# Stacked float32r products for a rank 32 term, with a tile of parts for each pair of heads

## The chip, the cores and the metric

One Trainium2 chip, one of its cores. The metric is the device time of one execution of the program in microseconds (us), the median over runs.

## The reference

Three layers follow one another; B = 4 sequences of S = 576 tokens, 512 features (8 heads of 64). The change touches the second line of the second layer.

```python
# 1: attention with a window of 128, ALiBi bias, per head
scores = where(mask, q @ k.T / 8 + bias, -1e9)
x = softmax(scores) @ v                       # [4, 576, 512]
# 2: low rank mix over the tokens, then a channel MLP
xt = x.transpose(0, 2, 1)
u = x + (xt @ U @ V).transpose(0, 2, 1)       # U [576, 32], V [32, 576]
x = u + maximum(u @ w_ch1, 0) @ w_ch2         # 512 -> 2048 -> 512
# 3: gated MLP
h = maximum(x @ w_in, 0); a, g = split(h)
out = (a * (w_spatial @ layernorm(g) + b_spatial)) @ w_out
```

## The kernel before, in words

Everything is written as tasks of a planner (`Plan`, L147): a task names its engine or a choice of engines, a cost, a priority and what it reads and writes. `run` (L216) lays the tasks out on TensorE (PE), VectorE (DVE), ScalarE (ACT), GpSimd (POOL) and the DMA queue of SP eight times, with priorities taken from the layout before, and emits the order that its own costs call the shortest. So a task that is added anywhere in the attention part can move the tasks around it on every engine, and a task with a choice (L599 `minus`, L413 `copy`, the normalisation at L1079) can change its engine. Within an engine the emitted order is the order of execution. Tiles live in rings of buffers (L109); a new tile of a ring waits for all users of the buffer's last tile.

The attention part goes through the sequences b = 0 to 3 and through four pairs of heads in each. `heads` (L996) loads q and k, computes scores (L1044), maximum and exponentials (L1055 on DVE, L1060 on ACT), normalises (L1080 on POOL or L1082 on DVE), transposes (L1090) and multiplies with v (L1128). `turned` (L1143) transposes the result once more (L1155). `low_rank` (L1162) then adds the low rank term to the sequence's tiles `u[b][pair]`, which hold features in the partitions and tokens in the columns:

- the mix (L1171) computes U^T x: 20 float32 products per sequence, whose results stand in one PSUM tile `t`, 32 rows for each pair;
- one copy (L1176, carried out at L416) brings `t` into the SBUF tile `th`;
- `up` (L1181) multiplies with V. `v32` holds V in each of the four groups of 32 rows, so that the products of all four pairs run at the same time in four groups of rows of the array (mode "quarter rows"). V's 576 columns are done in two halves of 288; the four products of one half are one task, here called a block. Each product is float32, which the trace shows as two instructions;
- VectorE adds each result to `u[b][pair]` (L1189).

In sequence 0 this is done for pairs 0 and 1 first, and later for pairs 2 and 3 (four half blocks, of two products each); in sequences 1 to 3 for all four pairs at once (two blocks each). The results lie in the PSUM rings `sc` and `at`, three buffers each (one more each in sequence 0); `t` is a buffer of `at` too.

`low_rank_weights` (L974) loads U and V as 64 bit words, turns them into float32 with five operations (L452 to L465) and spreads V over the rows with four DMAs (L983).

While attention is still going on, TensorE is filled with the first quarter of the channel MLP for the first 1536 tokens (`early_group`, L555): L545 to L547 for the first weight matrix, L584 to L586 for the second. These are float32r: each operand is split into a high and a low part that float32r holds exactly, and three products (high x high, low x high, high x low) stand for one. The three lines are called a triple. When attention is done its pool of SBUF is given back, and the casts (L529, ACT) and subtractions (L532, POOL) for the other tokens of that quarter may write there; their first product is L545 with 384 columns.

Of the kernel before, what the change touches and what calls it, by code (L numbers as in the profile page):

```python
# [338 lines left out]
def tile_kernel(ctx, tc, qT, kT, v, U, V, w1, w2, w_in, wspT, bsp, w_out, bias, out):  # L339
    nc = tc.nc  # L340
# [82 lines left out]
    def engines(kind, usual):  # L423
        return BOTH if kind in K["flex"] else (usual,)
# [512 lines left out]
    def constant(name, shape, dtype):  # L937
        return Ring(in_att, name, 1).new(shape, dtype)
# [25 lines left out]
    for p in ps:  # L964
        for t in (0, 8):
            P.add("POOL", 0.1, lambda p=p, t=t: nc.gpsimd.memset(p[:, REST[t] * 128 + 64 : REST[t] * 128 + 128], 0.0),
                  w=[p.part("zero")], prio=-1)
    r_xt, r_th = Ring(in_att, "xt", 2), Ring(in_att, "th", 2)


    u32 = constant("u32", [128, 5, RANK], F32)
    v32 = constant("v32", [128, S], F32)

    def low_rank_weights(prio, early, prio_v, early_v):  # L974
        single(u32, [(0, block(U, 0, 128, 0, RANK)), (1, block(U, 64, S, 0, RANK, 4))], 5, RANK, prio, None, early)
        P.add("DVE", 0.1, lambda: nc.vector.memset(u32[64:, 0], 0.0), w=[u32], prio=prio)
        n = S // 2
        v4 = constant("v4", [128, 1, n], F32)
        single(v4, [(0, block(V, 0, RANK, i // 2 * n, i // 2 * n + n), slice(RANK * i, RANK * i + RANK)) for i in range(4)],
               1, n, prio_v, None, early_v)  # L980
        for q in range(2):
            for d in range(2):
                P.dma(64, n, lambda q=q, d=d: nc.sync.dma_start(  # L983
                    out=v32[64 * d : 64 * d + 64, q * n : q * n + n], in_=v4[64 * q : 64 * q + 64, 0]),
                    r=[v4], w=[v32.part((q, d))], prio=K["vc"])

    vl = {}
    spare = r_f1.new([128, 128], F32)
# [173 lines left out]
    def low_rank(b, xts, pairs, p0):  # L1162

        sc, tp = (r_sc0, r_at0) if b == 0 else (r_sc, r_at)
        rows = slice(pairs[0] * 32, pairs[-1] * 32 + 32)
        t, th = tp.new([128, 128], F32), r_th.new([128, 128], F32)

        def mix():
            for c in range(5):
                for pair in pairs:  # L1170
                    nc.tensor.matmul(t[pair * 32 : pair * 32 + 32], u32[:, c], xts[pair // 2][:, c, pair % 2],  # L1171
                                     start=c == 0, stop=c == 4, skip_group_check=True)

        P.add("PE", 5 * 4 * 128 / 2400 + 0.1, mix, r=[u32] + [xts[h].part(c) for h in {p // 2 for p in pairs} for c in (0, 2, 4)],
              w=[t], prio=p0, mode="quarters")
        copy(engines("t", "ACT"), 128, lambda: th[rows], lambda: t[rows], PSUM, r=[t], w=[th], prio=p0 + 0.05)  # L1176
        for s0 in (0, 288):
            sl = slice(s0, s0 + 288)
            outs = [(sc, tp)[pair % 2].new([128, 288], F32) for pair in pairs]

            def up(sl=sl, outs=outs):  # L1181
                for pair, o in zip(pairs, outs):
                    d = slice(pair * 32, pair * 32 + 32)
                    nc.tensor.matmul(o.ap(), th[d], v32[d, sl], start=True, stop=True)

            P.add("PE", 4 * 288 / 2400 + 0.1, up, r=[th] + list(v32.parts.values()), w=outs, prio=p0 + 0.1, mode="quarter rows")
            for pair, o in zip(pairs, outs):
                ub = u[b][pair]
                P.add("DVE", dve(288), lambda o=o, ub=ub, sl=sl: nc.vector.tensor_tensor(  # L1189
                    out=ub[:, sl], in0=o.ap(), in1=ub[:, sl], op=ALU.add),  # L1190
                    r=[o], w=[ub.part(0), ub.part(1), ub], prio=p0 + 0.2)
# [544 lines left out]
```

## Time and profile before

| | us |
|---|---|
| median of 3 runs | 714.22 (714.04 to 715.3) |
| the profiled execution, its own time | 713.79 |
| its span, first to last instruction | 712.0 |
| TensorE busy | 701.7 (99%) |
| VectorE busy | 576.0 (81%) |
| ScalarE busy | 394.0 (55%) |
| GpSimd busy | 75.0 (11%) |

The granted TensorE clock is 1.00 over the span. PE is the matmul side of TensorE, PEld its weight loads; matmuls are pipelined and their recorded ends overlap the next one's start, so a product's price is read from start to start. VectorE's rows overlap in the same manner by a little.

### The profile page before, as it was taken

What the parts mean: (1) busy time and instruction counts of PE and PEld (TensorE: products, weight loads), DVE (VectorE), ACT (ScalarE), POOL (GpSimd) and SP (SyncE); (2) the same over time, 40 slices, a digit from 0 to 9 for tenths busy, and PEclk for the clock granted to TensorE, in tenths of its full rate; (3) what the DMA queues carried; (4) which work ended last, traced back from release to release, by engine and by line L of the source; (5) the groups of instructions that cost most, each with busy time, mean ns of one, the idle gap of its engine ahead of it and who ended that gap; (6) DMA issues with size and microseconds to landing.
All of it is one profiled execution on the core that took longest, in us unless ns stands there. A gap on an engine that the chain in (4) does not pass through costs nothing.

```text
span 712.0 us, 14829 instructions
## 1 busy us (share of the span) xinstructions
PE 701.7 (99%) x5434; PEld 637.8 (90%) x5434; DVE 576.0 (81%) x1637; ACT 394.0 (55%) x1082; POOL 75.0 (11%) x114
## 2 busy tenths in 40 slices
PE   8989999999999999999999999999999999999998
PEld 6767778778799999999999999999998898898896
DVE  6999996775597999999695998696589989859561
ACT  7878666564353655547253562544267566566352
POOL 2243330310400000000000000040010100100000
DMA  8865212210074166628475555447694202100102
GB/s 233 280 221 161 66 52 82 72 53 2 1 225 157 42 228 220 223 106 267 149 225 175 168 195 185 144 148 264 239 386 174 80 30 68 54 22 0 60 1 75
DMA packets 58799, 98.48 MB, mean 138 GB/s; under 512 B 8357, under 2 KB 38309, under 8 KB 58726
## 3 DMA queue, kind: packets, MB, share of 16 engines
q1 hardware_dynamic: 58437, 97.23, 41.2%
q8 instruction: 43, 0.70, 0.4%
q14 instruction: 31, 0.25, 0.1%
q10 hardware_dynamic: 288, 0.30, 0.1%
HBM read 67.67 MB, written 29.54 MB: 137 GB/s over the span
## 4 chain that ended last, share of the span: by engine, by line
PE 88%; DVE 7%; ACT 2%; DMA 1%; issue 1%; POOL 0%; SPq 0%; POOLq 0%; ACTq 0%
PE sc L586 8%; PE sc L584 8%; PE sc L585 8%; PE at L885 6%; PE at L886 6%; PE at L887 6%; PE at L1128 3%; PE sc L1044 2%; PE sc L1423 2%; PE sc L1421 2%; PE sc L1422 2%; PE at L1090 2%; PE at L1423 2%; PE at L1421 2%; PE at L1422 2%; PE acc L584 2%
## 5 line engine op out<-in xcount | busy, mean ns | idle before, releaser
L584 PE MATMUL sc<-h,wa 128*128 128x384 f32 (+1 forms) x328 | 110.6, 337 | 0.0
L585 PE MATMUL sc<-h,wa 128*128 128x384 f32 (+1 forms) x328 | 110.5, 337 | 0.0
L586 PE MATMUL sc<-hl,wa 128*128 128x384 f32 x320 | 108.7, 340 | 0.0
L1060 ACT ACTIVATE p<-p,nmax 128x192 f32<-128x192 f32 (+2 forms) x144 | 61.5, 431 | 10.2 <-DVE nmax L1055 10.0
L584 PEld LDWEIGHTS sc<-h,wa 128*128 128x128 f32 x328 | 61.6, 188 | 0.3
L585 PEld LDWEIGHTS sc<-h,wa 128*128 128x128 f32 x328 | 61.5, 187 | 0.3
L933 DVE TENSOR_TENSOR y<-sc,y 128x384 f32<-128x384 f32 (+1 forms) x96 | 40.7, 450 | 25.6 <-PE sc L586 25.3
L885 PE MATMUL at<-xd,wa 128*128 128x384 f32 x180 | 60.9, 338 | 0.0
L886 PE MATMUL at<-xd,wa 128*128 128x384 f32 x180 | 60.8, 338 | 0.0
L887 PE MATMUL at<-xd,wa 128*128 128x384 f32 x180 | 60.8, 338 | 0.0
L586 PEld LDWEIGHTS sc<-hl,wa 128*128 128x128 f32 x320 | 60.1, 188 | 0.0
L1055 DVE CUSTOM_DVE_ANT_0 p<-sc,bias 128x192 f32<-128x192 f32 (+2 forms) x144 | 40.3, 328 | 12.7 <-PE sc L1044 12.4
L905 ACT COPY c<-at 128x384 f32<-128x384 f32 x54 | 25.8, 478 | 39.2 <-PE at L887 38.9
L416 ACT CAST wa<-st 128x256 fp32r<-128x256 f32 (+1 forms) x62 | 28.1, 475 | 25.2 <-DVE st L465 13.1
L897 ACT ACTIVATE h<-c 128x384 fp32r<-128x384 f32 x54 | 28.4, 526 | 19.7 <-DVE c L892 19.5
L892 DVE TENSOR_TENSOR c<-at,c 128x384 f32<-128x384 f32 x54 | 29.8, 551 | 8.2 <-PE at L887 4.9
L885 PEld LDWEIGHTS at<-xd,wa 128*128 128x128 f32 x180 | 33.8, 188 | 0.0
L886 PEld LDWEIGHTS at<-xd,wa 128*128 128x128 f32 x180 | 33.8, 188 | 0.0
L887 PEld LDWEIGHTS at<-xd,wa 128*128 128x128 f32 x180 | 33.8, 188 | 0.0
L1044 PE MATMUL sc<-kr,qr 64*64 64x192 f32 (+2 forms) x576 | 31.7, 319 | 1.2 <-DMA qr<-in_qT 0.7
L1090 PE MATMUL at<-ident,p 128*128 128x128 f32 x208 | 31.1, 281 | 1.5 <-DVE p L1082 1.4
L1090 PEld LDWEIGHTS at<-ident,p 128*128 128x128 f32 x208 | 23.0, 140 | 10.4 <-issue 3.3
(407 smaller groups left out, 2007.7 us busy)
## 6 DMA issues: line engine op xcount, KB each, us to landing
wa<-in_w SPq DMA_DIRECT2D x32, 512.0 KB, 4.3
xd<-formsa SPq DMA_DIRECT2D x24, 192.0 KB, 3.0
qr<-in_qT SPq DMA_DIRECT2D x15, 288.0 KB, 3.3
kr<-in_kT SPq DMA_DIRECT2D x15, 288.0 KB, 4.0
vr<-in_v SPq DMA_DIRECT2D x16, 256.0 KB, 4.3
raw<-in_w_in SPq DMA_DIRECT2D x8, 512.0 KB, 3.9
kepts<-raw SPq DMA_DIRECT2D x14, 288.0 KB, 2.1
out<-h SPq DMA_DIRECT2D x15, 256.0 KB, 2.0
```

The lines of the kernel that those rows point to most:

```text
L584: nc.tensor.matmul(o, wt[:, 0, 0, c], hh[:, j], start=i == 0 and x == 0, stop=False, skip_group_check=True)
L585: nc.tensor.matmul(o, wt[:, 1, 0, c], hh[:, j], start=False, stop=False, skip_group_check=True)
L586: nc.tensor.matmul(o, wt[:, 0, 0, c], hl[:, j], start=False, stop=i == len(wts) - 1, skip_group_check=True)
L885: nc.tensor.matmul(o.ap(), wh()[:, k], xh.ap(), start=start and k == 0, stop=False, skip_group_check=True)
L886: nc.tensor.matmul(o.ap(), wl()[:, k], xh.ap(), start=False, stop=False, skip_group_check=True)
L887: nc.tensor.matmul(o.ap(), wh()[:, k], xl.ap(), start=False, stop=k == 1, skip_group_check=True)
L892: P.add("DVE", dve(N3), lambda: nc.vector.tensor_tensor(out=out.ap(), in0=ps_.ap(), in1=sb.ap(), op=ALU.add), r=[ps_, sb], w=[out], prio=0)
L933: P.add("DVE", dve(m), lambda acc=acc, dst=dst, s=s, m=m, o=o: nc.vector.tensor_tensor(out=dst[:, s : s + m], in0=acc[:, 0, o : o + m], in ...
L1044: nc.tensor.matmul(s[o : o + 64, c0 : c0 + k1 - k0], qr[d, 64 * t : 64 * t + 64], kr[d, k0:k1], start=True, stop=True, skip_group_check=True)
L1055: nc.vector.tensor_tensor_reduce(out=o(), in0=s[:, c0 : c0 + nk], in1=bias_t[:, pair, t % 2, 192 - nk :], scale=-0.125, scalar=BIG, op0=AL ...
L1060: nc.scalar.activation(out=o(), in_=o(), func=AF.Exp, scale=-1.0, bias=nmax[:, sl, t : t + 1], accum_out=sums[:, sl, t : t + 1])
L1090: P.add("PE", 0.109, lambda pt=pt, n_=n_, s0=s0: nc.tensor.transpose(pt[:, n_ - s0], p[:, n_ * 128 : n_ * 128 + 128], ident), r=[p.part(t) ...
```

## The change

V is split into a high and a low float32r part, and `v32` now holds high, high, low, low in its four groups of 32 rows (32 rows are one copy of V's 32 rows). Each pair has a tile `four[pair]` of 128 x 128 of its own, cleared once: the high part of its 32 x 128 mix in two of the groups, the low part in a third, and zeros in the fourth, so that one float32r product over all 128 rows sums high x high, high x low and low x high. The copies (two of 32 rows for each pair, on ACT or DVE) and the subtraction (DVE) read `t` in PSUM and write other groups of rows than they read. The product of each pair and half is a task of its own in the ordinary mode.

```diff
-    r_xt, r_th = Ring(in_att, "xt", 2), Ring(in_att, "th", 2)
+    r_xt, four = Ring(in_att, "xt", 2), [constant(f"four{pair}", [128, 128], F32R) for pair in range(4)]
+    for part in four:
+        P.add("POOL", 0.12, lambda part=part: nc.gpsimd.memset(f32(part.ap()), 0.0), w=[part], prio=-1)
...
-    v32 = constant("v32", [128, S], F32)
+    v32 = constant("v32", [128, S], F32R)
...
-        v4 = constant("v4", [128, 1, n], F32)
+        v4, v4h = constant("v4", [128, 1, n], F32), Ring(in_left, "y", 0, more=["y_4"]).new([128, n], F32R)
...
+        P.add("ACT", act(n, 0.09), lambda: nc.scalar.copy(out=v4h.ap(), in_=v4[:, 0]), r=[v4], w=[v4h], prio=K["vc"])
+        minus(("DVE",), n, lambda: v4[:, 0].bitcast(F32R), lambda: v4[:, 0], lambda: f32(v4h.ap()), r=[v4h], w=[v4], prio=K["vc"])
         for q in range(2):
-            for d in range(2):
-                P.dma(64, n, lambda q=q, d=d: nc.sync.dma_start(
-                    out=v32[64 * d : 64 * d + 64, q * n : q * n + n], in_=v4[64 * q : 64 * q + 64, 0]),
-                    r=[v4], w=[v32.part((q, d))], prio=K["vc"])
+            for d, (src, t) in enumerate(((lambda: f32(v4h.ap()), v4h), (lambda: v4[:, 0], v4))):
+                P.dma(64, n, lambda q=q, d=d, src=src: nc.sync.dma_start(
+                    out=f32(v32[64 * d : 64 * d + 64, q * n : q * n + n]), in_=src()[64 * q : 64 * q + 64]),
+                    r=[t], w=[v32.part((q, d))], prio=K["vc"])
...
-        copy(engines("t", "ACT"), 128, lambda: th[rows], lambda: t[rows], PSUM, r=[t], w=[th], prio=p0 + 0.05)
+        strip = lambda g: slice(32 * g, 32 * g + 32)
+        for pair in pairs:
+            part, low = four[pair], 0 if pair == 1 else 1
+            def highs(copy_, pair=pair, part=part):
+                for to in (pair, 2 if pair < 2 else 0):
+                    copy_(out=part[strip(to)], in_=t[strip(pair)])
+            P.either([("ACT", 0.53, lambda highs=highs: highs(nc.scalar.copy)), ("DVE", 0.6, lambda highs=highs: highs(nc.vector.tensor_copy))],
+                     r=[t], w=[part], prio=p0 + 0.05)
+            P.add("DVE", 0.3, lambda pair=pair, low=low, part=part: nc.vector.tensor_tensor(
+                out=part[strip(low)], in0=t[strip(pair)], in1=f32(part[strip(pair)]), op=ALU.subtract), r=[t], w=[part], prio=p0 + 0.05, lat=0.2)
         for s0 in (0, 288):
             sl = slice(s0, s0 + 288)
-            outs = [(sc, tp)[pair % 2].new([128, 288], F32) for pair in pairs]
-            def up(sl=sl, outs=outs):
-                for pair, o in zip(pairs, outs):
-                    d = slice(pair * 32, pair * 32 + 32)
-                    nc.tensor.matmul(o.ap(), th[d], v32[d, sl], start=True, stop=True)
-            P.add("PE", 4 * 288 / 2400 + 0.1, up, r=[th] + list(v32.parts.values()), w=outs, prio=p0 + 0.1, mode="quarter rows")
-            for pair, o in zip(pairs, outs):
-                ub = u[b][pair]
+            for pair in pairs:
+                o, ub = (sc, tp)[pair % 2].new([128, 288], F32), u[b][pair]
+                P.add("PE", mm(288), lambda pair=pair, o=o, sl=sl: nc.tensor.matmul(o.ap(), four[pair].ap(), v32[:, sl], start=True, stop=True),
+                      r=[four[pair]] + list(v32.parts.values()), w=[o], prio=p0 + 0.1)
```

How the order moves, at three places. The lines of the change lie a few further down: its L1195 is the product that was L1184, its L1197 the add that was L1189, its L1185 and L1189 the copies and the subtraction of the parts, its L1086 the normalisation that was L1082.

PE in sequence 1, the first block of the low rank term; before (`acc`, `sc` and `at` are PSUM tiles, `wa` weights, `h` the hidden layer):

```order
L586 MATMUL acc<-h,wa 128x512
L1184 MATMUL sc<-v_441,th 128x288
L1184 MATMUL at<-v_441,th 128x288
L1184 MATMUL sc<-v_441,th 128x288
L1184 MATMUL at<-v_441,th 128x288
L584 MATMUL acc<-h,wa 128x512
```

The same place in the change (`four_97`, `four_94`, `four_101` and `four_104` belong to pairs 0, 1, 2 and 3):

```order
L1195 MATMUL sc<-v_490,four_97 128x288
L584 MATMUL acc<-h,wa 128x512
L585 MATMUL acc<-h,wa 128x512
L586 MATMUL acc<-h,wa 128x512
L1195 MATMUL at<-v_490,four_94 128x288
L1195 MATMUL sc<-v_490,four_101 128x288
L1195 MATMUL sc<-v_490,four_97 128x288
L1195 MATMUL at<-v_490,four_104 128x288
L1195 MATMUL at<-v_490,four_94 128x288
L1195 MATMUL sc<-v_490,four_101 128x288
L1195 MATMUL at<-v_490,four_104 128x288
L584 MATMUL acc<-h,wa 128x512
```

The two blocks with triples between them have become eight products, the first alone and seven in a row. Between the mix and the first of them there are three triples in the change, four in sequence 2 and three in sequence 3, where there were two, one and one.

DVE in sequence 0, ahead of the last adds of its low rank term; before (`p_77` holds the probabilities, `ph`, `xt` copies of transposes, `st` weights):

```order
L417 COPY xt<-at 128x512
L1068 RECIPROCAL rinv<-rinv 128x9
L458 TENSOR_SCALAR st<-st 128x512
L1082 TENSOR_SCALAR p_77<-p_77,rinv 128x192 x4
L1082 TENSOR_SCALAR p_77<-p_77,rinv 128x64
L1082 TENSOR_SCALAR p_77<-p_77,rinv 128x192 x3
L1082 TENSOR_SCALAR p_77<-p_77,rinv 128x128
L459 TENSOR_SCALAR st<-st 128x512
L1189 TENSOR_TENSOR u<-sc,u 128x288
```

The same place in the change:

```order
L417 COPY xt<-at 128x512
L417 COPY xt<-at 128x256
L1072 RECIPROCAL rinv<-rinv 128x9
L1086 TENSOR_SCALAR p_77<-p_77,rinv 128x192 x3
L1086 TENSOR_SCALAR p_77<-p_77,rinv 128x64
L1086 TENSOR_SCALAR p_77<-p_77,rinv 128x128
L1185 CAST four_104<-at 32x128 x2
L1189 TENSOR_TENSOR four_101<-at,four_101 32x128
L1189 TENSOR_TENSOR four_104<-at,four_104 32x128
L1086 TENSOR_SCALAR p_77<-p_77,rinv 128x192
L1197 TENSOR_TENSOR u<-sc,u 128x288
```

Three of the nine normalisations are POOL's now, L458 and L459 come later, and two copies and two subtractions of the parts stand in their place (as many stand at the first half of the sequence).

PE at the end of attention, from the last block of sequence 3 on; before:

```order
L1184 MATMUL sc<-v_441,th 128x288
L1184 MATMUL at<-v_441,th 128x288
L1184 MATMUL sc<-v_441,th 128x288
L1184 MATMUL at<-v_441,th 128x288
L584 MATMUL acc<-h,wa 128x512
```

The same place in the change:

```order
L1195 MATMUL at<-v_490,four_94 128x288
L1195 MATMUL sc<-v_490,four_101 128x288
L584 MATMUL sc<-h,wa 128x512
L585 MATMUL sc<-h,wa 128x512
L586 MATMUL sc<-h,wa 128x512
L1195 MATMUL at<-v_490,four_104 128x288
L584 MATMUL sc<-h,wa 128x512
```

Behind the last row of the low rank term there were eleven triples up to the first product of 384 columns, and now there are seven.

## Rows read from the trace of the kernel before

**Rows 1.** Busy time (and instructions) by stage: stage, PE, PEld, DVE, ACT, POOL, PEclk, DMA, GB/s.

```profile
25.00:50.00 25.00, 22.26 (x377) 16.03 (x378) 24.32 (x93) 20.14 (x66) 9.90 (x8) 1.00 0.77 259
50.00:75.00 25.00, 24.47 (x308) 18.88 (x307) 25.00 (x88) 19.83 (x65) 9.84 (x14) 1.00 0.52 155
100.00:200.00 100.00, 99.76 (x1143) 79.27 (x1134) 67.97 (x256) 52.83 (x178) 20.00 (x32) 1.00 0.15 49
```

**Rows 2.** Waits of PE, 0 to 100 us: us in total, times, longest.

```profile
PE at L1090 <- DVE p L1082: 1.4, 2, 1.0
```

**Rows 3.** Timeline of PE, sequence 1, first block: start, us, engine, line, operation.

```profile
88.39 0.40 PE L585 MATMUL acc<-h,wa 128*128 128x512 f32 x1
88.63 0.39 PE L586 MATMUL acc<-h,wa 128*128 128x512 f32 x1
...
89.64 0.50 PE L584 MATMUL acc<-h,wa 128*128 128x512 f32 x1
```

**Rows 4.** Timeline of PE, sequence 3 and the end of attention.

```profile
182.69 0.47 PE L584 MATMUL acc<-h,wa 128*128 128x512 f32 x1 [0.24 <-PE at L1184]
...
184.26 0.49 PE L584 MATMUL acc<-h,wa 128*128 128x512 f32 x1
...
191.88 0.34 PE L545 MATMUL at<-xd,wa 128*128 128x384 f32 x1
```

**Rows 5.** Timeline of PE, float32r products of 288 columns late in the kernel.

```profile
640.42 0.29 PE L1574 MATMUL at<-wf,x 128*128 128x288 f32 x1
...
641.34 0.29 PE L1574 MATMUL sc<-wf,x 128*128 128x288 f32 x1
```

**Rows 6.** Groups of ACT by form, 0 to 200 us: xcount, busy us, mean ns, idle.

```profile
L416 ACT COPY th<-at 128x128 f32<-128x128 f32 x3 | 0.8, 267 | 3.8 <-PE at L1171 3.8
```

**Rows 7.** Groups of DVE by form, 0 to 200 us.

```profile
L1082 DVE TENSOR_SCALAR p<-p,rinv 128x192 f32<-128x192 f32 x70 | 22.9, 381 | 0.1
L417 DVE COPY ph<-at 128x384 f32<-128x384 f32 x22 | 11.6, 547 | 2.6 <-PE at L1090 2.6
...
L417 DVE COPY ph<-at 128x512 f32<-128x512 f32 x11 | 7.5, 683 | 0.0
L1189 DVE TENSOR_TENSOR u<-sc,u 128x288 f32<-128x288 f32 x16 | 7.2, 449 | 0.8 <-PE at L1184 0.8
...
L458 DVE TENSOR_SCALAR st<-st 128x512 f32<-128x512 f32 x10 | 4.8, 494 | 0.0
...
L417 DVE COPY xt<-at 128x256 f32<-128x256 f32 x3 | 1.3, 422 | 0.1
...
L594 DVE TENSOR_TENSOR y<-sc,u 128x128 f32<-128x128 f32 x2 | 0.6, 292 | 3.9 <-PE sc L586 3.9
```

**Rows 8.** Timeline of DVE around a memset of partitions 64 to 127.

```profile
26.34 0.08 DVE L1055 DVE_READ_ACCUMULATOR2_ANT nmax<- 128x1 f32 x1
26.48 0.09 DVE L976 MEMSET u<- 64x32 f32 x1
26.60 0.36 DVE L1055 CUSTOM_DVE_ANT_0 p<-sc,bias 128x192 f32<-128x192 f32 x1
```

**Rows 9.** POOL at the end of attention: timeline row (merged), then the group by form.

```profile
185.02 8.43 POOL L532 TENSOR_TENSOR x<-u,xd 128x192 fp32r<-128x192 f32 x12 [27.79 <-ACT xd L529]
...
L532 POOL TENSOR_TENSOR x<-u,xd 128x192 fp32r<-128x192 f32 x8 | 4.5, 603 | 27.8 <-ACT xd L529 27.8
```

**Rows 10.** Timeline of PE, sequence 0: a half block, and the first dense product.

```profile
30.50 0.51 PE L1184 MATMUL sc<-v,th 32*128 32x288 f32 x1
...
31.67 0.87 PE L1090 MATMUL at<-ident,p 128*128 128x128 f32 x6
...
48.75 0.50 PE L545 MATMUL f<-x,wa 128*128 128x512 f32 x1
```

**Rows 11.** Timeline of ACT, the first exponential.

```profile
4.83 0.35 ACT L1060 ACTIVATE p<-p,nmax 128x64 f32<-128x64 f32 x1 [1.68 <-DVE nmax L1055]
```

**Rows 12.** Timeline of SP's queue, the last DMAs of V.

```profile
22.20 1.11 SPq L983 DMA_DIRECT2D v<-v  x2
```

More of the change, by code (lines that the diff above doesn't have):

```diff
@@ L1164, in low_rank @@
         sc, tp = (r_sc0, r_at0) if b == 0 else (r_sc, r_at)
-        rows = slice(pairs[0] * 32, pairs[-1] * 32 + 32)
-        t, th = tp.new([128, 128], F32), r_th.new([128, 128], F32)
+        t = tp.new([128, 128], F32)
         def mix():
```

## The prediction

> **What bounds the kernel now.** I read the busy time by stage first, then the waits, then the timelines of the stretches that the change touches. By stage [rows 1], TensorE has work for 22.26 of the 25 us from 25 to 50 us, when sequence 0 is finished, and for 24.47 of 25 us after that; from 100 to 200 us it is busy 99.76 of 100. VectorE is the full one early: 24.32 of 25 us, then 25.00 of 25, and only 67.97 of 100 later. The reader is to see two regimes: up to about 75 us VectorE decides when things are ready and TensorE waits a little; from there on TensorE's own work is the time, and a us of it saved is a us of the kernel. The waits of TensorE in the first 100 us say the same: the longest row is transposes that wait for VectorE's normalisation, 1.4 us in two waits [rows 2]. The low rank term lies in both regimes: four half blocks (of two pairs each) in sequence 0, two full blocks in each of sequences 1, 2 and 3.
>
> **Sequences 1 to 3: the products on TensorE.** A block now is four products at once, one in each group of 32 rows, in float32. Between two ordinary 512 column products it takes the place from 88.63 to 89.64 us, 1.01 us, of which 0.24 (88.39 to 88.63) is the ordinary product's own [rows 3]: 0.77 us for a block, the change of mode before and behind it included. There are six such blocks, and one of them is followed by a 0.24 us stall [rows 4]: 6 x 0.77 + 0.24 = 4.86 us. The change replaces each block by four float32r products of 128 rows and 288 columns. Such products exist late in the kernel with a new weight tile each: seven of them take 0.92 us (640.42 to 641.34), 0.131 us each [rows 5]. 24 x 0.131 = 3.15 us. They run in the mode of their neighbours. Gain 1.71 us, all in a stretch where TensorE is the bound.
>
> **What stands between mix and product there.** One copy on ScalarE (0.267 us [rows 6]) becomes, per pair, two copies of 32 rows and a subtraction, and the order puts two pairs' copies on ScalarE, two on VectorE, all four subtractions on VectorE: eight small operations there. The trace has no 32 x 128 operation. The nearest is the 128 x 128 add from PSUM, 0.292 us [rows 7]; behind one another such operations overlap by about 0.08, so 0.21 us is the lower price. The upper one comes from the one VectorE operation that starts at another partition than its neighbours, the memset at 26.48 us: it lasts 0.09 but takes from 26.42, when the read before it ends, to 26.60 [rows 8], so 0.06 us stand ahead of it where other rows overlap. That makes 0.292 + 0.06 = 0.35. Eight cost 1.7 to 2.8 us. TensorE covers them: three of the triples L584 to L586 (four in sequence 2) stand between the mix and the first product now, instead of one or two: nine products at 0.23, 2.1 us. I take a wait of 0.05 us each in sequences 1 and 3, 0.1 in all, since most of the eight run beside ScalarE's copies and before the cover ends; the bounds are 0 and 0.7 each.
>
> The Trainium skill (VectorE: DVE Perf Modes, section Two Vector instructions with no wait between them) speaks against the change here: an operation whose input or output starts in another group of 32 partitions than the last one's is held until everything before it has finished. The memset row agrees, once. By that rule the eight cost 2.8 us rather than 1.7, and the sum would lose the 0.7 us in two sequences.
>
> The eight products per sequence need eight PSUM buffers and the two rings have six, but the adds that free them take 0.449 us or less [rows 7] and the first one frees its buffer before the seventh product; I cost that at nothing, 0.4 us a sequence as the bound.
>
> **The end of attention.** The casts for the next stage may only write when the last low rank product has run. Now the last block ends before 184.26 us, eleven triples follow, and the next stage's first product comes at 191.88 [rows 4]. In the change only seven triples follow, 4.8 us. GpSimd's eight subtractions of 192 columns, 0.603 us each [rows 9], are 4.8 us, and they began 0.76 us behind the block's end, at 185.02 [rows 9]: 5.6 us. That looks 0.8 us short, but the first product needs only the first of the eight tiles, and the last is wanted by the twelfth, 11 x 0.17 = 1.9 us later (0.17 is 0.23 scaled to 384 columns). So 1.1 us are spare: cost nothing, bound +0.8.
>
> **Sequence 0.** Two half blocks behind one another take 1.17 us (30.50 to 31.67 [rows 10]); all four are 2.34. Eight products at 0.131 are 1.05: TensorE has 1.29 us less to do. What it collects depends on VectorE. Added ahead of the last add of the sequence: eight small operations (1.7 to 2.8) and the low part of V, priced as the 288 column add, 0.449 less the overlap, 0.37: 2.1 to 3.2 us. Taken away ahead of the same add, by counting both orders: three normalisations of 192 columns, now GpSimd's (3 x 0.30), a 384 and two 512 column copies against two of 256 (1.0 net), one L458 and one L459 that now come later, both at L458's price (0.8): 2.7 us, every duration less 0.08 [rows 7]. Net -0.6 to +0.5, so the last add comes when it came. ScalarE gets the casts (four of 0.267 for two [rows 6], and one of V, taken like VectorE's 0.449) and the copies VectorE gave up, some 2 us where 4.9 of 25 are idle [rows 1]. GpSimd's three normalisations lie ahead of the two subtractions that feed the first dense product, in place of a weight split that moves behind them. The 0.8 us of L458 and L459 come back after 50 us, where VectorE is full. I take zero for sequence 0; the bounds are -1.3 (TensorE collects all) and +3.2 (VectorE pays all that was added).
>
> The four memsets on GpSimd, 1.2 us at the 0.292 of the add, lie ahead of what the first exponential reads; ScalarE is idle for 1.68 us before that one, until VectorE's row maximum [rows 11], so they are covered up to that. V's four DMAs stay four; the last two are issued from 22.20 to 23.31 us [rows 12] and V is first read at 30.50 [rows 10], so a cast and a subtraction ahead of them are covered; the loads behind them on SP's queue wait no longer than those two.
>
> **Sum.** -1.71 + 0.1 + 0 + 0 = -1.6 us. The profiled execution took 713.79, so 712.2 by its own time; it stands 0.43 below the median of 714.22, so I forecast **712.6 us** against the median. A measurement of this kernel tells about 0.2%, 1.43 us, from no change.
>
> **The rivals.**
> B, sequence 0 pays too. For it: no idle time stands in front of the first dense product at 48.75 us [rows 10], which TensorE reaches in its own order, so shorter blocks may bring that forward. Against it: VectorE has 24.32 of 25 us there. -1.71 - 1.29 = -3.0: 711.2 us.
> C, the gain is waited away. Waits behind the mix (0.7 in two sequences), PSUM (0.4 in three) or the end of attention (0.8), or the new order of everything around them, take 0.6 to 1.6 us back: about 713.7 us, no change. For it: eight small operations stand where one copy stood. Against it: the triples that the order put between.
> D, slower: VectorE's early queue decides. The eight operations are held at 0.35 and the removed work comes back in the full stretch after 50 us, so the first dense product is late by 3.2 + 0.8 = 4.0 us; with 1.7 gained later that is +2.3: 716.5 us. For it: VectorE busy 25.00 of 25 us [rows 1]. Against it: the order moved 2.7 us away from ahead of the last add. It decides once the first product L545 begins later than 48.75 + 1.7 + 1.4 = 51.9 us.
> E, the products stay at four passes. Two half blocks are eight instructions, two at a time: four steps of 1.17 / 4 = 0.29 us [rows 10], and a product takes two. Unstacked that is 0.58 a product, 24 x 0.58 = 13.9 against 4.86, +9.1: 723.3 us. Against it: the 0.131 of the same type and shape [rows 5].
>
> The Trainium skill (TensorE: Matmul & The Clock Gate, Part 3: Packing small matmuls) measures 3.07 times the speed for four packed products of 32 rows, which speaks against giving the packing up; for products that kept their passes a block would by that be 0.77 x 3.07 = 2.4 us. No run here shows it yet, and the row of 0.131 decides otherwise.
>
> **How the numbers follow.** Forecast 0.40, B 0.15, C 0.24, D 0.18, E 0.03. The forecast's own range is 711.9 to 713.3, and some three quarters of it lie more than 1.43 us under the median. So faster: 0.15 + 0.30 = 0.45; same: 0.10 + 0.24 = 0.34; slower: 0.21. The range takes in the forecast and C, nearly all of B and the nearer part of D; it leaves out E, the farther part of D (0.12) and the end of B (0.04): 710.9 to 715.9.
>
> **What would show it.** Low rank products about 0.13 apart and no change of mode around them: the first term. The gap from mix to first product filled with triples and no idle time: the second. First product L545 within 1 us of 48.75: sequence 0 at nothing; near 47.5 is B, past 51.9 is D. TensorE idle in front of the first 384 column product, or in the low rank blocks: C. Small VectorE operations above 0.35 us apart, or products 0.5 us apart, would make my prices wrong; a change of the time that arises behind 200 us would make the account itself wrong.

## The result and the profile after

| | before | after |
|---|---|---|
| median, us | 714.13 (713.65 to 715.3, 6 runs) | 720.03 (718.44 to 720.32, 6 runs) |
| the profiled execution, its own time | 713.79 | 719.27 |
| its span | 712.0 | 717.3 |
| first product of 384 columns | 191.88 [rows 4] | 196.37 |

The change is slower: ratio 1.0077, interval 1.0064 to 1.0090. The forecast was 712.6, the range ended at 715.9. Of the six executions of the change, the four whose mean granted clock was 0.994 or 0.995 took 719.94 to 720.32 us, the two at 0.999 and 1.000 took 719.27 and 718.44; the profiled one is one of these two, so that 5.9 us between the medians are 5.3 between the spans. Of the 5.3 us between the spans, 4.5 have arisen by the first product of 384 columns, 0.8 behind it.

The stages that answer to [rows 1], after (stage, PE, PEld, DVE, ACT, POOL, clock, DMA, GB/s):

```profile
25.00:50.00 25.00, 21.36 (x375) 15.91 (x373) 24.34 (x90) 20.07 (x66) 10.24 (x10) 1.00 0.80 265
50.00:75.00 25.00, 22.54 (x245) 17.38 (x244) 24.91 (x89) 20.91 (x70) 10.83 (x14) 1.00 0.53 156
75.00:100.00 25.00, 22.47 (x286) 17.46 (x285) 21.95 (x75) 13.71 (x45) 7.70 (x11) 1.00 0.16 48
100.00:200.00 100.00, 99.11 (x1193) 79.61 (x1192) 71.63 (x283) 56.19 (x199) 23.83 (x42) 1.00 0.15 46
```

PE was busy 24.47 of 25 us from 50 to 75 us [rows 1] and now is 22.54; from 25 to 50 us it has lost 0.9 us more. In 100 to 200 us it lost 0.65 [rows 1]. From 75 to 100 us it lost 2.06, by the row of the kernel before:

```profile
75.00:100.00 25.00, 24.53 (x324) 17.98 (x327) 23.80 (x83) 16.85 (x62) 8.61 (x13) 1.00 0.24 70
```

The loss is early: about half of it from 25 to 75 us, where VectorE is full, and a good third from 75 to 100 us, where it is not. PE's waits, 0 to 100 us, the view of [rows 2] (us in total, times, longest):

```profile
PE sc L1048 <- DVE nmax L1059: 2.6, 3, 1.7
PE at L1159 <- DVE u L1139: 1.1, 1, 1.1
PE at L1094 <- DVE p L1086: 1.0, 1, 1.0
PE sc L1195 <- DVE four L1189: 1.0, 2, 0.6
PE at L1132 <- DVE ph L417: 0.9, 1, 0.9
```

Only the fourth row is a wait for the new parts. The others are waits of the attention part for VectorE: for the row maximum, the scaling of the products with v, the normalisation, a copy. Not all of them come from the parts. In e9 below, the same order with the parts left out, the second row is gone, but the first, third and fifth stand there with 2.0, 1.1 and 0.9 us: those are not the parts'.

Sequence 1's low rank term, after, answers to [rows 3] (timeline of PE, ACT and DVE: start, us, engine, line, operation, idle before and until what):

```profile
89.38 1.30 PE L1174 MATMUL at<-xt,u 128*32 128x128 f32 x40
90.74 0.52 ACT L1185 CAST four<-at 32x128 fp32r<-32x128 f32 x2 [2.10 <-PE at L1174]
91.29 0.60 DVE L1185 CAST four<-at 32x128 fp32r<-32x128 f32 x2 [0.52 <-ACT four L1185]
91.93 0.53 ACT L1185 CAST four<-at 32x128 fp32r<-32x128 f32 x2 [0.67 <-DVE four L1185]
92.49 0.62 DVE L1185 CAST four<-at 32x128 fp32r<-32x128 f32 x2 [0.59 <-ACT four L1185]
93.12 1.24 DVE L1189 TENSOR_TENSOR four<-at,four 32x128 fp32r<-32x128 f32 x4
93.55 0.37 PE L1195 MATMUL sc<-v,four 128*128 128x288 f32 x1 [0.60 <-DVE four L1189]
...
95.09 0.29 PE L1195 MATMUL sc<-v,four 128*128 128x288 f32 x1
95.86 0.40 PE L1195 MATMUL at<-v,four 128*128 128x288 f32 x1 [0.48 <-DVE u L1197]
96.46 0.50 PE L584 MATMUL acc<-h,wa 128*128 128x512 f32 x1 [0.20 <-DVE y L594]
```

The reader is to see four things. **ACT and DVE take turns.** Each pair's copies begin when the other engine's pair is done, though the pairs are different rows of `t`. From 90.74 to 94.36 the eight copies and four subtractions run one at a time: 3.6 us. Three triples (2.1 us) cover it only in part, and PE waits 0.60. The eighth product then waits 0.48 for a PSUM buffer, and the next triple 0.20 for an add to `y` that stands behind the adds to `u`. The waits on the tiles `four`, over all sequences, say the same (whose engine sat idle, until what):

```profile
  ACT four L1185: 3.7, 6
  DVE four L1185: 2.0, 3
```

5.7 us of ACT's and DVE's time is waiting for each other's part copies. By the trace's semaphore events the first copy of such a group on DVE waits for ACT's copies, and the next group on ACT for DVE's. The copies of different pairs write different tiles; what they share is the one PSUM tile `t`, and where the same copies read an SBUF tile (e13 below) the turns are gone. The Trainium skill (PSUM — Partial Sum Buffer, section PSUM bank collisions raise a hardware error) asks for a guard between two engines by bank and by group of 32 partitions, and says that different groups of one bank do not collide. By that rule pairs in different groups would need no turns. No run here takes the turns away on the PSUM tile itself, so that stays untried.

The marks that the prediction named, after (PE):

```profile
49.62 0.50 PE L545 MATMUL f<-x,wa 128*128 128x512 f32 x1
55.54 0.56 PE L1048 MATMUL sc<-kr,qr 64*64 64x192 f32 x8 [1.66 <-DVE nmax L1059]
196.37 0.34 PE L545 MATMUL at<-xd,wa 128*128 128x384 f32 x1
```

The first dense product is only 0.87 late, and no idle time stands ahead of the first product of 384 columns. VectorE's own work has become longer too (timeline of DVE and POOL, then a group by form):

```profile
34.66 1.27 POOL L532 TENSOR_TENSOR x<-u,x 128x512 fp32r<-128x512 f32 x1 [0.59 <-ACT x L529]
34.86 1.35 DVE L458 TENSOR_SCALAR st<-st 128x512 f32<-128x512 f32 x1
...
L458 DVE TENSOR_SCALAR st<-st 128x512 f32<-128x512 f32 x10 | 6.5, 659 | 0.0
```

L458 takes 494 ns in the mean before [rows 7] and 659 now, 1.7 us over its ten. With the parts left out (e9) it takes 543, so about 1.2 us are owed to the parts. This one started while GpSimd's subtraction ran and ended 0.28 us after it.

### The profile page after: what moved, and what is told of

Same layout as the page of the kernel before. It is cut to its first block, busy times and chain, and to the rows that moved or that the text cites. A ratio compares the mean times of both kernels' runs of the same rounds, so it can differ in the third digit from the quotient of the medians.

```text
span 717.3 us, 14817 instructions
## 1 busy us (share of the span) xinstructions
PE 700.4 (98%) x5402; PEld 640.5 (89%) x5402; DVE 581.0 (81%) x1661; ACT 396.7 (55%) x1093; POOL 81.1 (11%) x128
## 4 chain that ended last, share of the span: by engine, by line
PE 65%; DVE 7%; DMA 1%; issue 0%; ACT 0%; DVEq 0%; ACTq 0%
PE sc L586 7%; PE sc L584 7%; PE sc L585 7%; PE at L885 5%; PE at L886 5%; PE at L887 5%; PE sc L1431 2%; PE sc L1430 2%; PE sc L1429 2%; PE at L1431 2%; PE at L1430 2%; PE at L1429 2%; DVE xd L602 1%; PE at L546 1%; PE sc L1582 1%; PE at L545 1%
## 5 line engine op out<-in xcount | busy, mean ns | idle before, releaser
L1132 PEld LDWEIGHTS at<-ph,vr 128*64 128x64 f32 (+1 forms) x960 | 24.9, 136 | 8.6 <-ACT ph L416 2.2
```

## The experiments

A product moved by the planner changes the order everywhere, so most of the runs hold the order fixed: `run` (L216) is replaced by a table that says which task is emitted when and on which engine. The groups of runs had medians of the kernel before from 713.97 to 714.18.

| run | operations | order | median | ratio to before, interval | first 384 |
|---|---|---|---|---|---|
| e2 | before | change | 715.90 | 1.0024, 1.0013 to 1.0034 | 193.81 |
| e9 | change, no parts | change | 714.31 | 1.0001, 0.9991 to 1.0011 | 192.51 |
| e13 | change, parts from SBUF | change | 715.99 | 1.0032, 1.0019 to 1.0045 | 193.67 |
| e8 | change, no parts | before | 712.55 | 0.9981, 0.9972 to 0.9990 | 190.66 |
| e1 | change | before, products moved | 731.37 | 1.0246, 1.0220 to 1.0273 | 208.82 |

**Order against operations.** e1 and e2 emit one kernel's tasks in the other's order:

```diff
-        for t, t.eng, t.cost, t.emit, t.start in min(plans)[2]:
+        for code in np.frombuffer(zlib.decompress(base64.b85decode(ORDER)), np.uint16):
+            t = self.tasks[int(code) & 4095]
...
             t.emit()
```

> The change's operations, all of them, emitted in the order of the kernel before: every task that both kernels have keeps its place and its engine; the new ones stand where the old copy, the old blocks and the old DMAs stood, except that the products of sequences 1 to 3 stand two to three triples further back. Theory 'order' (the planner's new order of everything up to 100 us lost the time, the change's own terms are as summed): 712.0 to 714.0 us, PE idle in 50 to 100 us about 1 us as before [rows 1]. Theory 'parts' (the copies and subtractions cost it, in whatever order they stand): 717 to 720 us, PE idle of 3 us or more in front of the low rank products and behind their adds.

Measured: 731.37. Neither theory has that number. In the old order there is no room for the parts: PE waits 2.8 us for them in three waits, 3.0 us for adds queued behind them, and 3.7 us for one `y`. It also shows what waiting does to the clock (stages, then a row of PE):

```profile
43.00:45.00 2.00, 0.44 (x2) 0.20 (x3) 1.89 (x9) 0.48 (x1) 0.00 (x0) 1.00 1.02 394
45.00:46.00 1.00, 0.97 (x4) 0.92 (x5) 0.97 (x5) 0.00 (x0) 0.00 (x0) 0.57 0.35 129
46.00:47.00 1.00, 1.00 (x7) 0.98 (x6) 0.97 (x3) 0.00 (x0) 0.00 (x0) 0.50 0.11 41
...
46.15 1.91 PE L1093 MATMUL at<-ident,p 128*128 128x128 f32 x8
```

After two us in which PE worked 0.44, the granted clock is 0.50, the 1.2 GHz level, and eight transposes take 1.91 us. So this run is a bad measure of the parts alone. It says that an order and the operations that it was made for belong together.

> The operations of the kernel before, all of them, emitted in the order of the change: every task that both have at the change's place and on the change's engine (three more normalisations of sequence 0 on POOL among them); each old block stands where the first of its four or two products stands in the change, the old copy where the first part is copied. Theory 'order': 718 to 721 us, PE idle 4 to 5 us from 50 to 100 us as in the change. Theory 'parts': 713.5 to 715.5 us, and PE idle there 1 to 2 us.

Measured: 715.90, above "parts" and below "order". The new order alone costs 1.8 to 1.9 us, a third of the loss. The first dense product comes at 48.07, ahead of the kernel before (48.75 [rows 10]), and the first product of 384 columns at 193.81, behind it (191.88 [rows 4]): the order loses its time between the two. Here are PE's wait for the row maximum, with 0.92 where the change has 1.66, and L457, the line that is L458 there, with its plain duration:

```profile
53.24 0.56 PE L1043 MATMUL sc<-kr,qr 64*64 64x192 f32 x8 [0.92 <-DVE nmax L1054]
...
L457 DVE TENSOR_SCALAR st<-st 128x512 f32<-128x512 f32 x10 | 4.5, 456 | 0.0
```

With the old operations the order keeps this line at 4.5 us. With the change's operations but without parts (e9) the same ten take 5.4, with the parts, which make VectorE later still, 6.5.

**The parts on one engine, and another order of the change.**

```diff
-            P.either([("ACT", 0.53, ...), ("DVE", 0.6, ...)], r=[t], w=[part], prio=p0 + 0.05)
+            P.either([("DVE", 0.6, ...)], r=[t], w=[part], prio=p0 + 0.05)
```

> The change in its own order, with one thing moved: all part copies are VectorE's, pair by pair (two copies, then the subtraction of the same pair), so that ACT and VectorE no longer take turns at the PSUM tile t. In the profile of the change ACT and DVE wait 5.7 us for each other's part copies, and PE 1.6 us for the subtractions. Theory 'order': 718.5 to 720.5, hardly a change, since those waits are a small part of the loss; PE's wait at the products falls from 1.6 to under 0.6 us. Theory 'parts', by the turns at t: 716 to 718 us. Theory 'parts', by VectorE's work: 720.5 to 723 us, since 16 copies of 0.28 us more stand on VectorE.

Measured: 720.96 (ratio 1.0100, 1.0082 to 1.0119), in the last of the ranges. No turns are left, and yet nothing is won: the chain is as long on one engine, in sequence 1 from 92.13 to 95.90, and VectorE has more to do. One at a time costs the same whoever does it.

```profile
92.13 0.59 DVE L1184 CAST four<-at 32x128 fp32r<-32x128 f32 x2
...
95.61 0.29 DVE L1188 TENSOR_TENSOR four<-at,four 32x128 fp32r<-32x128 f32 x1
```

> The change in another one of the eight orders that its planner lays out (the fourth in place of the one chosen); the operations are the same. Theory 'order': the time differs from the change's 720.0 by more than 1 us, either way, 714 to 724, and the difference lies in PE's idle time ahead of 100 us. Theory 'parts': 719 to 721 us, since each order holds the same parts.

The edit is `plans[3]` for `min(plans)`. Measured: 720.38 (1.0089, 1.0069 to 1.0110), so a second order of the change is as slow, as "parts" had it.

**The parts left out.** The tasks stay in the plan and in their order and emit nothing:

```diff
             def highs(copy_, pair=pair, part=part):
+                if b == 0:
+                    return
...
-            P.add("DVE", 0.3, lambda pair=pair, low=low, part=part: nc.vector.tensor_tensor(
+            P.add("DVE", 0.3, lambda pair=pair, low=low, part=part: b == 0 or nc.vector.tensor_tensor(
```

> The change in its own order, the copies and subtractions of the parts left out in sequence 0 alone (four pairs: eight copies, four subtractions; its products read what the cleared tiles hold, so sequence 0 lacks its low rank term). Everything else stays in place. Theory 'parts' (the small operations and the turns that ACT and VectorE take at them hold up VectorE's full early stretch): 716 to 718 us, the first L545 at 48 us or earlier in place of 49.62, and less PE idle from 50 to 75 us than the change's 2.5. Theory 'order' (the 1.9 us that the order alone cost, and nothing of the parts): 719 to 720.5 us. Theory 'late parts' (the loss of the parts lies in sequences 1 to 3): 719 to 720.5 us as well, and told apart by the next run.

Measured: 716.92 (1.0042, 1.0025 to 1.0059), 3.1 less than the change: "parts". Where sequence 0 pays is seen from the same product on, first in the change (PE):

```profile
26.88 1.76 PE L1132 MATMUL at<-ph,vr 128*64 128x64 f32 x60 [0.32 <-ACT ph L416]
...
39.20 1.10 PE L1159 MATMUL at<-ident,u 128*128 128x128 f32 x6 [1.13 <-DVE u L1139]
```

Then in e5 (PE, DVE, PE):

```profile
25.83 1.76 PE L1132 MATMUL at<-ph,vr 128*64 128x64 f32 x60 [0.30 <-ACT ph L416]
...
33.13 0.42 DVE L458 TENSOR_SCALAR st<-st 128x512 f32<-128x512 f32 x1
...
46.50 0.50 PE L545 MATMUL f<-x,wa 128*128 128x512 f32 x1
```

Without its parts sequence 0 brings L458 to VectorE at 33.13, ahead of GpSimd's subtraction at 33.25; it takes 0.42 where it took 1.35, and the wait of 1.13 for `u` behind it is gone. To the first dense product it is 20.67 us in place of 22.74 (49.62 - 26.88): 2.1 us, all ahead of that product. The other 1.0 between these two executions stands already at the product at 25.83, before any part runs; in e9, with the same work up to there, it comes at 26.97.

> The change in its own order, the copies and subtractions of the parts left out in sequences 1 to 3 (their products read the parts that sequence 0 left, so their low rank term is that of sequence 0's mix). Theory 'parts' in sequence 0: 717.5 to 719 us, since PE's waits at the products and behind them in sequences 1 to 3 sum to 2.2 us in the change's trace (0.60, 0.48, 0.20, 0.28, 0.60) and some of it comes back. Theory 'late parts': 715 to 717 us. Theory 'order': 719.5 to 720.5 us.

Measured (`b > 0` in the edit): 716.17 (1.0031, 1.0020 to 1.0043), 3.9 less: "late parts" as well. Both halves pay. In the traces it is 104.05 us from the mix of sequence 1 to the first product of 384 columns here (89.80 to 193.85) and 106.99 in the change (89.38 to 196.37), 2.9 more, of which PE's waits of 0.60, 0.48, 0.20, 0.28 and 0.60 are 2.2.

> The change in its own order with the copies and subtractions of the parts left out in all sequences (the low rank term is missing). It closes the sum: leaving them out in sequence 0 gave 716.9 (-3.1), in sequences 1 to 3 716.2 (-3.9). If the two prices add up: 712.5 to 713.5 us. If one stall hid behind the other: 714 to 716 us. Beside the kernel before in this same order (715.9) it is also what the stacked products give in this order: 1.5 us as in the order of before, or up to 3.0 by the sum with sequence 0.

Measured (both left out): 714.31. Without the parts the change is level with the kernel before; with them it loses 5.7 us. The two prices, 3.1 and 3.9, come to 1.3 more than that, about what the interval of e5 alone leaves open (1.2 us either way). The traces have 2.1 in sequence 0, 2.9 from the mix of sequence 1 to the first product of 384 columns, as in e6, and 0.4 behind it: 5.4 us. Beside e2, the same order with the old operations, the stacked products give 1.6 us, the old copy of `t` left out with them. PE's longest wait of the change stands here as well, without any parts (PE, then a stage):

```profile
53.54 0.56 PE L1048 MATMUL sc<-kr,qr 64*64 64x192 f32 x8 [1.66 <-DVE nmax L1059]
...
55.00:60.00 5.00, 5.00 (x20) 3.90 (x19) 4.22 (x14) 2.88 (x11) 2.82 (x4) 0.66 0.94 243
```

In this execution the granted clock fell behind that wait. It is 0.66 in the mean of these 5 us; products of 512 columns come 0.43 us apart (56.42 to 56.85) where they are 0.23 apart at 1.00. By 72.54, the fourth group of dense products, that has cost 1.0 us beside the change's execution, whose clock stayed at 1.00 behind the same wait (24.92 us from the first dense product, 23.88 there). With it the spans, 713.0 and 717.3, differ by 4.3 and not by 5.4. So such a wait of PE can cost more than itself, in some executions.

> The change's operations in the order of the kernel before, with the copies and subtractions of the parts left out everywhere (the low rank term is missing; the products run on cleared tiles at the places of the old blocks). So it holds the first term of the sum alone: stacked products for blocks. If 24 products at 0.131 us for six blocks at 0.77 and the stall are right: 711 to 712.6 us (1.7 us from sequences 1 to 3, and up to 1.3 more from sequence 0). If the stacked products give PE nothing: 713.5 to 715 us. Against the first run of this order with the parts in (731.4 us) the difference is the price of parts placed where one copy stood.

Measured: 712.55, 1.5 us below the kernel before. That is the first term of the sum, with the old copy of `t` left out too. The first dense product comes at 48.89, no earlier than before (48.75 [rows 10]), so the gain lies behind sequence 0. Against e1 the parts cost 18.8 us in this order. A block of the stacked form in that run (PE):

```profile
88.97 0.30 PE L1195 MATMUL sc<-v,four 128*128 128x288 f32 x1
89.11 0.29 PE L1195 MATMUL at<-v,four 128*128 128x288 f32 x1
89.24 0.29 PE L1195 MATMUL sc<-v,four 128*128 128x288 f32 x1
89.38 0.29 PE L1195 MATMUL at<-v,four 128*128 128x288 f32 x1
89.51 0.39 PE L583 MATMUL acc<-h,wa 128*128 128x512 f32 x1
```

Four products take 0.54 us where a block took 0.77 [rows 3]; they are 0.13 apart.

**The parts from SBUF.** One copy brings `t` to SBUF, and the parts read that, on the engines and at the places that they had:

```diff
+        copy(("ACT",), 128, lambda: th[rows], lambda: t[rows], PSUM, r=[t], w=[th], prio=p0 + 0.05)
...
-                    copy_(out=part[strip(to)], in_=t[strip(pair)])
+                    copy_(out=part[strip(to)], in_=th[strip(pair)])
```

> The change in its own order, with one float32 copy of t to SBUF on ACT added ahead of each sequence's parts; the parts read that copy, on the engines and at the places they had, so no two engines take turns at a PSUM tile. Theory 'turns' (ACT and DVE waiting 5.7 us for each other's part copies made the parts late): 717.5 to 719 us, DVE waits at the part copies under 1 us. Theory 'VectorE's queue' (twelve small operations among VectorE's own work, whichever way they are handed over): 719.5 to 721 us.

Measured: 715.99, 4.0 less than the change and lower than even "turns" had it. Sequence 1 in that run:

```profile
89.86 0.27 ACT L415 COPY th<-at 128x128 f32<-128x128 f32 x1 [2.12 <-PE at L1174]
90.16 1.26 ACT L1186 CAST four<-th 32x128 fp32r<-32x128 f32 x4
90.16 0.95 DVE L1186 CAST four<-th 32x128 fp32r<-32x128 f32 x4 [0.27 <-ACT th L415]
91.14 1.23 DVE L1190 TENSOR_TENSOR four<-th,four 32x128 fp32r<-32x128 f32 x4
91.94 0.30 PE L1196 MATMUL sc<-v,four 128*128 128x288 f32 x1
```

The copies of both engines begin at 90.16 together. From the first copy to the last subtraction it takes 2.5 us in place of 3.6, an operation more included, and PE does not wait ahead of the first product. DVE's waits at the part copies are 1.1 us, both for the one copy, where "turns" had under 1. Two more things differ from the change: VectorE's casts are shorter from SBUF (below), and `v4` lies in another buffer; their share was not measured. In sequence 2 VectorE's four casts take 1.73 us instead of 0.95, beside GpSimd's normalisations (3.67 us from 136.37).

> The change with the parts taken off VectorE: one float32 copy of the PSUM tile t to SBUF on ACT, from there all part copies on ACT and all subtractions on GpSimd; the planner lays out its own order. If the price of the parts is VectorE's work and the turns at t: 714 to 717 us. If it is the way from mix to product on whatever engine: 719 to 722 us, with PE waiting for GpSimd's subtractions where it waited for VectorE's.

The edit to e13's form gives all copies to ACT and the subtractions to `nc.gpsimd`. Measured: 716.89 (1.0037, 1.0024 to 1.0050), with another order of the planner: within the first range.

**Another form**, split but not stacked (from the kernel before):

```diff
+        P.add("DVE", dve(128), lambda: nc.vector.tensor_tensor(out=tl[rows], in0=t[rows], in1=f32(th[rows]), op=ALU.subtract),
+              r=[t, th], w=[tl], prio=p0 + 0.05)
...
-                    nc.tensor.matmul(o.ap(), th[d], v32[d, sl], start=True, stop=True)
+                for n_, (w, x) in enumerate(((th, v32), (th, v32l), (tl, v32))):
...
+                        nc.tensor.matmul(o.ap(), w[d], x[d, sl], start=n_ == 0, stop=n_ == 2)
```

> Another form, from the kernel before: the mix of all pairs stays in the four groups of rows of one tile, its high part (one copy) and its low part (one subtraction) are two tiles, V's high and low part stand in four groups each, and a block is three float32r products for each pair (high x high, high x low, low x high), four pairs at a time in the four groups of rows. Two operations of 128 x 128 stand between mix and products in place of twelve small ones; V takes eight DMAs for four. Theory 'parts': PE gains about a quarter of each block's 0.77 us, 6 x 0.2 = 1.2, and 0.3 x 4 = 1.2 in sequence 0; the one subtraction (0.29) is covered: 711.5 to 714.0 us. Theory 'order' (any new order of the early stretch costs some 2 us): 713.5 to 716 us. If float32r products of 32 rows do not run side by side, a block takes 12 x 0.131 = 1.57 us, and the time is 719 to 722 us.

> The form split in four groups of rows (two operations of 128 x 128 between mix and products, three float32r products side by side) emitted in the order of the kernel before; its subtraction stands behind the copy, its DMAs at the places of the old ones. In its own order it took 715.1, with 0.70 us for a block (91.48 to 92.18) where the kernel before takes 0.78. Theory 'order' (the 1.0 us above the kernel before is the planner's new order): 712.8 to 713.8 us, by 6 x 0.08 + 0.24 + some of sequence 0. Theory 'split' (the split itself, its longer way from mix to product, costs it): 714.5 to 716 us.

Measured: 715.10 (1.0014, 1.0004 to 1.0024) in its own order, 715.63 (1.0020, 1.0011 to 1.0030) in that of before. The products do run side by side, three steps a block. The first run fits "order", but in the old order the form is no faster, so the range of "split" is the right one. Its eight DMAs and its split of V lie in the stretch where VectorE is full; which of its parts costs the time was not tried.

**Is the rest the order?** Both forms in orders found by the same search (single tasks of the first 200 us moved, by the planner's costs). In a first pair of runs the clearing of the softmax's row sums stood behind its first use, so their output was another one: 713.73 (1.0005, 0.9990 to 1.0021) and 714.12 (1.0007, 0.9992 to 1.0023). With the clearing at the front:

> The stacked form with parts read from an SBUF copy of t, in the searched order, with the clearing of the row sums moved back to the front. Theory 'order': as the run before it, 712.5 to 714.5 us, so 2 us below the same operations in the change's order (716.0). Theory 'form': 715 us or more.

> The same operations in a second order, found by the same search from another start of its random numbers, which the planner's costs hold for 1.5 us longer than the first. Theory 'order': 711 to 716 us, unlike the first by more than 0.5 us. Theory 'form': 715 to 717 us.

> The kernel before in its searched order, with the clearing of the row sums at the front. Theory 'order': 712.5 to 715 us; the stacked form is ahead only if the first run of this group lies below this one by more than 0.7 us.

Measured: 715.05 (1.0011, 0.9999 to 1.0022) and 714.96 (1.0009, 0.9999 to 1.0018) for the stacked form with parts from SBUF, 714.18 (1.0009, 1.0000 to 1.0017) for the kernel before. The first is just in the range of "form"; the second differs from it by 0.1, not by the 0.5 that "order" asked for. An order can give back about 1 us of the 2.0 that e13 still lies above the kernel before; no run of the stacked form that does all its work came out ahead of it.

## Why the prediction was wrong

By the runs in the change's order the loss is a sum: the new order +1.8 (e2 against before), the stacked products -1.6 (e9 against e2), the parts +5.7 (change against e9). That makes +5.9, as it must, since each run is held against the one before it. What supports the terms is that they come out alike elsewhere: the products give 1.5 in the other order (e8), and the order costs 1.8 with the change's products too (e9 against e8).

- **The products on TensorE: right.** -1.71 forecast for sequences 1 to 3; -1.5 and -1.6 measured, sequence 0 included. Rival B, by which sequence 0 would gain 1.29 more, is out for the old order (e8: 48.89 for 48.75). In the new one some 0.9 of the 1.6 lie there (20.65 us to the first dense product in e9, 21.57 in e2), so that the sum is about right and its place is not.
- **What stands between mix and product: the step that failed.** The price of one small operation was right: they are 0.31 apart, between my 0.21 and 0.35. The count was not. I set VectorE's eight against the cover and let ScalarE's four run beside them. But both engines read one PSUM tile, and in this program they went at it one at a time, so all twelve stand in one row: 3.6 us, some 2.7 of them (90.74 to 93.40) ahead of the first product, against a cover of 2.1. PE's wait of 0.60 in sequences 1 and 3 lies inside my bound of 0.7; taken was 0.05. In all, the parts cost 5.7 us, by the traces 2.9 of them here, where the sum had 0.1.
- **The PSUM buffers: costed at nothing, also wrong.** 0.48 in sequence 1, and 0.20 there and 0.28 in sequence 2 for `y` queued behind the adds. It was the eighth product that waited, 0.48 against my bound of 0.4: an add of 0.449 us frees a buffer only when VectorE gets to it, and VectorE came late from the parts and had other work between the adds.
- **The end of attention: right.** No idle time ahead of the product at 196.37.
- **Sequence 0 at zero: wrong by 3.1 us (e5).** I added and took away durations of rows. The operations moved as counted, but the parts made VectorE late, it met GpSimd's subtraction, L458 took 1.35 us for 0.42, and PE waited 1.13 behind it; by the traces that is 2.1 of the 3.1. My mark hid it: the first dense product came within 1 us of 48.75, as it should at no cost, because the new order had brought it forward (48.07 in e2, 47.62 in e9) and the parts took that back. The wait of 1.66 at 55.54 is not their price; it is in e9 too.
- **The order of everything else: no term at all.** It stood only in rival C, with at most 1.6 us for all its causes together. Alone it is 1.8.
- **The rivals.** C had the right places (behind the mix, PSUM, the order) and let them add up to the gain and no further, though its own bounds, 1.4, 1.2 and 0.8, come to 3.4. D had the right engine and the right side, but its point of decision, 51.9, was not reached. E: the products are not at four passes.

Open: which of the planner's moves make the 1.8 us; why 0.8 us arise behind the first product of 384 columns (0.4 in e2, e9 and e13), none of them before 235 us, which by my own sign the account does not cover; why the parts from SBUF (e13) still cost 1.7 over no parts (e9); and the form with the turns taken away on the PSUM tile itself.

## What to carry to other kernels

Before operations are spread over two engines, see what they read: two engines that read one PSUM tile may be ordered one behind the other by the program, and then the whole chain, not the longer half, has to fit under the cover. A product that is 0.2 us cheaper is no gain if twelve small operations on a full engine stand in front of it. And where a planner lays the work out anew, the order needs a price of its own: emit the old operations in the new order and measure it.

## What the runs showed of the hardware

- VectorE's L458, from SBUF to SBUF, is held up where GpSimd's subtraction has begun before it: 1.35 us at 34.86, beside GpSimd's 34.66 to 35.93. In e5 it begins first, at 33.13 against 33.25, and takes 0.42. The Trainium skill (SBUF — State Buffer, section Who interferes with whom) calls it an exclusive lock on a shared pair of ports that the loser waits out; the row agrees, since L458 ends 0.28 us after GpSimd.
- The same cast of 32 x 128 takes VectorE 284 ns from PSUM and 220 from SBUF, ScalarE 257 from PSUM and 296 from SBUF (medians of sixteen each, of the change and of e13).
- Float32r products of 32 rows run side by side in four groups of rows like float32 ones. In e7 the third step begins 0.13 us behind the second, the time of one product of 128 rows (0.131 [rows 5]), and the block takes 0.70 us from the end of the product ahead of it:

```profile
91.25 0.40 PE L586 MATMUL acc<-h,wa 128*128 128x512 f32 x1
91.58 0.40 PE L1190 MATMUL sc<-v,th 32*128 32x288 f32 x1
...
91.82 0.29 PE L1190 MATMUL sc<-v32l,th 32*128 32x288 f32 x1
...
91.95 0.28 PE L1190 MATMUL sc<-v,tl 32*128 32x288 f32 x1
...
92.18 0.50 PE L584 MATMUL acc<-h,wa 128*128 128x512 f32 x1
```

At 0.13 a step, an estimate, three steps are 0.39 of these 0.70 (91.48 to 92.18, with 0.23 for the ordinary product). The rest lies where the mode changes: 0.10 ahead of the first product, 0.11 more in the first step than in the second, 0.10 behind the last. Four products in the ordinary mode have none of it (0.54 in e8), and three cheap packed passes gain little on two dear ones, 0.77 [rows 3].
